# Four small copies moved from ACT and DVE to SP's DMA queue, with a new written order for every engine

## The chip, the core and the metric

The kernel runs on one core of a Trainium2 chip. The core has TensorE (PE), VectorE (DVE), ScalarE (ACT), GpSimd (POOL) and SyncE (SP); each runs its own list of instructions in order, and they wait for one another by semaphores. POOL and SP issue DMA transfers, which 16 DMA engines carry out. The metric is the device time of one execution in microseconds (us), less is better. Before the change it is 137.15 us, the median of 3 runs (137.09 to 137.99).

## The reference

Eight batches, eight heads, 576 positions, head size 64. Attention with a sliding window of 128 and a bias that falls with distance, then a token mixer whose mixing matrix is made from its input:

```
scores = scale * q @ k.T                       # per batch and head
scores = where(0 <= i - j < 128, scores - slope[h] * |i - j|, -1e9)
x      = softmax(scores) @ v                   # heads side by side: x is 576 x 512 per batch
wq, wk = x @ w_q, x @ w_k                      # 576 x 64 each
mixed  = (wq @ wk.T / 8) @ x
out    = relu(mixed) @ w_out                   # 576 x 512 per batch, float32
```

## The kernel before

All work is cut into named steps, and the kernel's text `ORDER` lists 720 of them as `name:engine`, for PE with the PSUM bank that the step fills and in some places a number of filler matmuls. The list was written by a planner from an estimated duration of each step per engine (the `on` argument of `add`, pairs of occupancy and latency in us); when the kernel is built, the steps are simply emitted in this order, and each engine executes its own in that order. So `ORDER` sets which engine does a step that several could do, which bank it uses, and in what order POOL and SP issue transfers.

A batch b goes through these steps (the first number is the batch):

- Loads: Lq, Lk, Lv, Lt (rows 512 to 575 of q and k), weights Lwq, Lwk, Lwo, all by POOL, which casts float32 to float16 on the way; FQ0 and FQ1 are the first two loads, by SP, cast by CQ0 and CQ1. The `load` function makes a load wait until only about 6 us of estimated service lie ahead of it.
- TW, TN, TT: transpositions of q and k on PE, evicted by ETW, ETN, ETT on ACT or DVE.
- QK: scores of a group of heads and a block of keys into a pair of PSUM banks; EXP: the exponential, on ACT, 64 times; MUL: the product with the exponential of the bias (zero outside the window), on DVE. Five buffers hold exponentials (`NPT = 5`).
- PV: the product with v and a column of ones; X: division by the sum (a reciprocal and a product), on DVE.
- XT and EXT: x is transposed and evicted (XT.0 and XT.1 large, XT.2 the last 64 rows). WK, WQ: the two projections, evicted by EWK, EWQ.
- G: since (wq wk.T) x = wq (wk.T x), only G = wk.T x (64 x 512) is made. It comes out as 128 partitions x 256: the lower 64 partitions hold columns 0 to 255, the upper 64 columns 256 to 511. EG copies it to `gs`. GX makes `gx`, the same with the two halves of the partitions exchanged, in two copies of 64 x 256.
- MX.0 and MX.1 multiply with `gs`, MX.2 and MX.3 with `gx`; RM is the relu and the scale, on ACT or DVE; OUT.0 to OUT.4 are the products with w_out, EO their evictions, DO the stores, by POOL or SP. The first store of SP after the step HOLD waits until the fourth last load has landed.

GX is the step that the change moves. In the function `add_g` (lines 727 to 771) its body already has a branch for each engine:

```
for r in range(2):
    out_ap = gx_s[b % 2][64 * r:64 * r + 64, :]
    lo = slice(64 - 64 * r, 128 - 64 * r)
    if o.eng == "SP":
        hold(nc.sync.dma_start(out=out_ap, in_=gs_s[b % 2][lo, :]))
    ...
    else:
        cp(o.eng, out_ap, one(g.bank)[lo, 0:256])
```

ACT and DVE copy from PSUM (line 222 or 224 of `cp`), SP would copy from `gs` in SBUF by DMA. The other lines that matter: L608 is EXP, L621 MUL, L662 and L663 X, L775 and L777 RM on ACT and DVE, L228 and L230 the evictions of transpositions, L494 and L496 those of TW, L213 the loads, L216 the stores, L908 the filler matmuls.

Of the kernel before, what the change touches and what calls it, by code (L numbers as in the profile page):

```python
# [48 lines left out]
QK1.1.0:P:1 QK0.3.1:P:3:1:0 QK0.3.0:P:0 Lv0.0:G zerop:G MUL0.1.0:V MUL0.0.0:V Lv0.1:G Lv0.2:G
Lv0.3:G EXP0.3.1:A Lv0.4:G MUL0.3.1:V EXP1.0.0:A EXP0.3.0:A Lq2.1:G ones4:V TW1.1:P:3 PV0.0:P:2  # L50
ones3:G ETW1.1.1:A X0.0:V ETW1.1.0:A PV0.1:P:0:1:0 MUL0.3.0:V EXP1.1.0:A Lk2.1:G QK1.0.1:P:3
EXP1.0.1:A Lwk:G Lv1.0:G X0.1:V PV0.2:P:2 X0.2:V QK1.1.1:P:1 EXP1.1.1:A PV0.3:P:0 X0.3:V
QK1.2.0:P:3 EXP1.2.0:A Lq2.0:G Lk2.0:G PV0.4:P:2 QK1.2.1:P:1 XT0.0:P:0 EXP1.2.1:A Lv1.1:G
XT0.1:P:3 EXT0.1:A X0.4:V XT0.2:P:20 EXT0.2:A EXT0.0:V MUL1.0:V QK1.3.1:P:0 EXP1.3.1:A TW2.1:P:1
# [12 lines left out]
PV2.4:P:1 MX1.3:P:2 RM1.3:A X2.4:V QK3.0.1:P:3 EXP3.0.1:A Lv3.1:G Lv3.0:G Lk4.2:G Lt2.3:G
Lk4.3:G Lv3.2:G PV2.2:P:0 QK3.1.1:P:2 EXP3.1.1:A X2.2:V XT2.2:P:10 EXT2.2:V TN4.1.0:P:3
ETN4.1.0:V Lk5.0:G Lq5.2:G Lq5.0:G Lk5.1:G Lv3.3:G Lv3.4:G Lk5.2:G MX1.2:P:0 RM1.2:A Lv4.2:G
Lk5.3:G Lq5.1:G Lq5.3:G XT2.1:P:1 QK3.3.0:P:2 EXP3.3.0:A Lq6.1:G Lv4.3:G QK3.2.1:P:3 QK3.2.0:P:0  # L70
EXT2.1:V WK2:P:10 EWK2:V MUL3.0:V EXP3.2.0:A QK3.3.1:P:2 EXP3.3.1:A WQ2:P:11 EWQ2:A G2:P:10
# [1 line left out]
EO0.0:A Lk6.2:G Lv5.4:G Lk6.1:G MUL3.1:V MX2.0:P:3 MX2.1:P:0 TN4.0.0:P:2 RM2.1:A RM2.0:A
ETN4.0.0:V OUT1.2:P:10 MUL3.3:V MX2.3:P:2 RM2.3:A QK4.0.1:P:0 EXP4.0.1:A Lk6.0:G TN4.0.1:P:3
ETN4.0.1:V OUT0.2:P:11 EO0.2:A PV3.0:P:2 MX2.2:P:3 RM2.2:A EO1.2:V QK4.0.0:P:0 EXP4.0.0:A
OUT1.0:P:10 X3.0:V EO1.0:A MUL3.2:V PV3.1:P:2 X3.1:V QK4.1.1:P:3 EXP4.1.1:A TN4.1.1:P:0 Lv5.0:G
Lt3.0:G Lq6.3:G MUL4.0:V ETN4.1.1:A OUT0.1:P:10 TT2:P:2 QK4.1.0:P:3 ETT5:V ETT4:V EO0.1:A
EXP4.1.0:A Lq6.2:G Lv6.4:G Lv5.3:G Lv5.2:G PV3.2:P:0 Lv5.1:G OUT2.2:P:10 EO2.2:A X3.2:V Lt3.2:G
Lq7.1:G TN5.1.0:P:3 ETN5.1.0:V Lk7.1:G Lq7.0:G DO0.1:G Lt3.1:G QK4.2.0:P:2 QK4.3.0:P:0 Lk7.3:G
Lq7.3:G Lt3.3:G PV3.3:P:1 EXP4.2.0:A X3.3:V EXP4.3.0:A OUT1.1:P:30 Lk7.0:G EO1.1:A PV3.4:P:2  # L80
MUL4.1:V QK4.3.1:P:0 EXP4.3.1:A XT3.0:P:1 EXT3.0:A X3.4:V OUT1.4:P:30 EO1.4:A MUL4.3:V
QK4.2.1:P:0 EXP4.2.1:A TN5.0.0:P:2 ETN5.0.0:V MUL4.2:V XT3.1:P:1 EXT3.1:A XT3.2:P:31 EXT3.2:A
OUT0.3:P:30 EO0.3:V TN5.1.1:P:0 ETN5.1.1:A TN5.0.1:P:2 ETN5.0.1:A QK5.0.0:P:1 EXP5.0.0:A
WK3:P:31 EWK3:V PV4.3:P:0 X4.3:V QK5.0.1:P:2 PV4.2:P:3 X4.2:V EXP5.0.1:A QK5.3.0:P:1 EXP5.3.0:A
# [8 lines left out]
X5.2:V QK6.1.1:P:3 EXP6.1.1:A WQ4:P:10 XT5.0:P:2 EWQ4:V EXT5.0:A QK6.2.0:P:0 EXP6.2.0:A
MX4.2:P:1 RM4.2:V XT5.1:P:3 EXT5.1:V OUT3.0:P:20 EO3.0:V MX4.0:P:0 MX4.1:P:1 RM4.1:V RM4.0:A
QK6.0.1:P:3 EXP6.0.1:A OUT3.3:P:21 EO3.3:V MX4.3:P:1 RM4.3:A Lv6.1:G TT3:P:0 ETT6:V ETT7:A
WK5:P:30 EWK5:A QK6.2.1:P:1 EXP6.2.1:A Lv6.0:G QK6.3.0:P:0 TN7.0.0:P:2 MUL6.1:V ETN7.0.0:V
# [7 lines left out]
MX5.2:P:2 RM5.2:A QK7.1.1:P:3 DO1.0:G EXP7.1.1:A XT6.2:P:00 HOLD:S DO1.1:S DO3.0:S DO4.0:S
EXT6.2:V MUL7.3:V OUT3.4:P:01 QK7.1.0:P:2 QK7.2.0:P:1 EXP7.1.0:A MUL7.0:V XT6.0:P:3 EXT6.0:A
OUT5.1:P:00 EXP7.2.0:A MUL7.1:V EO3.4:A PV7.4:P:2 X7.4:V EO5.1:A MUL7.2:V OUT5.2:P:30 EO5.2:A
OUT5.0:P:10 EO5.0:A WK6:P:00 EWK6:A PV7.0:P:3 DO2.0:S DO1.4:S X7.0:V PV7.1:P:2 X7.1:V DO4.3:G
# [836 lines left out]
```

## Time and profile before

| | |
|---|---|
| median of 3 runs | 137.15 us |
| the profiled execution | 137.09 us |
| its span, first to last instruction | 135.1 us |
| granted TensorE clock, mean | 0.99 |
| instructions | 5503 |
| busy: PE, ACT, DVE, POOL | 93%, 86%, 82%, 75% of the span |
| DMA | 24.86 MB moved, mean 184 GB/s |

A page of the profile shows one execution: each engine's busy time, the span in 40 slices with the busy share in tenths, the chain of work that ended last, the costliest groups of instructions with their mean duration and the idle time ahead of them, and the DMA issues with the time to landing. The trace answers finer questions: busy time in chosen stretches, timelines of one engine, who waited for whom.

### The profile page before, as it was taken

The numbers are of one execution on the slowest core, as the hardware profiler recorded it, in microseconds if no ns is written. First come the engines' busy times: TensorE is split into PE (matmuls) and PEld (weight loads), VectorE is DVE, ScalarE is ACT, GpSimd is POOL, SyncE is SP. The second block draws the span as 40 slices with busy tenths as digits, with TensorE's granted clock in tenths as the row PEclk, the third lists the DMA queues.
The fourth block names the chain that finished last, engine by engine and source line by source line (L and its number), as shares of the span: only waits on it lengthen the run. The fifth ranks groups of instructions, "written<-read, shape, count | busy, mean of one in ns | idle before, by whom it ended". The sixth has DMA issues, their size and how long they took to land.

```text
span 135.1 us, 5503 instructions
## 1 busy us (share of the span) xinstructions
PE 125.2 (93%) x2351; PEld 82.2 (61%) x2351; DVE 110.5 (82%) x210; ACT 116.6 (86%) x185; POOL 101.6 (75%) x154
## 2 busy tenths in 40 slices
...
DVE  5764869999899998999899999889998899936140
ACT  3489989999999999999999999999998996775710
...
GB/s 115 164 188 164 182 158 182 181 160 171 161 184 155 160 158 148 147 153 146 150 148 142 139 140 142 193 181 183 208 154 27 292 227 377 363 351 90 227 378 171
DMA packets 92680, 24.86 MB, mean 184 GB/s; under 512 B 80241, under 2 KB 89201, under 8 KB 92657
## 3 DMA queue, kind: packets, MB, share of 16 engines
...
q14 instruction: 6, 0.04, 0.1%
...
## 4 chain that ended last, share of the span: by engine, by line
PE 54%; POOL 18%; DMA 15%; ACT 6%; issue 3%; POOLq 0%; ACTq 0%
PE pair L207 48%; DMA natp<-in_k_dram 8%; PE pair L210 6%; POOL natp L213 5%; DMA vt<-in_v_dram 5%; POOL vt L213 5%; POOL natt L213 5%; ACT pt L608 4%; DMA wout_sb<-in_moe_w_out_dram 2%; POOL vt L332 1%; ACT natp L222 1%; ACT xT L228 0%; POOL vt L334 0%; POOL wq_sb L213 0%; POOL wout_sb L213 0%
## 5 line engine op out<-in xcount | busy, mean ns | idle before, releaser
L608 ACT ACTIVATE pt<-pair 128x1024 f16<-128x1024 f32 x64 | 63.7, 1045 | 1.9 <-PE pair L207 1.6
L621 DVE TENSOR_TENSOR pt<-pt,bias 128x2048 f16<-128x2048 f16 (+1 forms) x36 | 38.7, 1099 | 4.1 <-ACT pt L608 4.0
L213 POOL DMA_DIRECT2D vt<-in_v_dram x40 | 36.9, 1020 | 2.6 <-DMA natp<-in_k_dram 1.9
L207 PE MATMUL pair<-wout_sb,rm 128*128 128x512 f16 (+1 forms) x160 | 36.0, 381 | 0.1
L213 POOL DMA_DIRECT2D natp<-in_k_dram x24 | 23.8, 1006 | 1.1 <-POOLq L928 0.8
L216 POOL DMA_DIRECT2D out_dram<-natp x15 | 9.2, 618 | 20.3 <-ACT natp L222 20.3
L207 PEld LDWEIGHTS <-pt 128*128 128x128 f16 x576 | 20.4, 97 | 6.6 <-issue 3.4
L207 PE MATMUL pair<-qkT 64*128 64x256 f16 (+3 forms) x352 | 23.6, 243 | 0.7 <-DVE xT L230 0.2
L207 PE MATMUL pair<-vt,pt 128*128 128x65 f16 x576 | 23.3, 193 | 0.3
L663 DVE TENSOR_TENSOR x<-pair,inv 128x512 f16<-128x512 f32 x32 | 22.1, 691 | 1.1
L213 POOL DMA_DIRECT2D natp<-in_q_dram x23 | 22.2, 1010 | 0.5 <-DMA vt<-in_v_dram 0.5
L207 PEld LDWEIGHTS <-rm 128*128 128x128 f16 (+1 forms) x160 | 12.2, 100 | 12.9 <-issue 1.7
L775 ACT ACTIVATE rm<-pair 128x576 f16<-128x576 f32 x25 | 15.9, 660 | 1.9 <-PE pair L207 1.8
L222 ACT COPY natp<-pair 128x512 f32<-128x512 f32 x24 | 14.0, 607 | 3.6 <-PE pair L207 3.5
L210 PEld LDWEIGHTS <-natp 128*64 128x64 f16 (+1 forms) x512 | 12.9, 102 | 5.4 <-issue 3.9
L207 PEld LDWEIGHTS <-qkT 64*128 64x128 f16 x352 | 11.6, 94 | 5.3 <-issue 2.2
L908 PE MATMUL pair<-fill 128*128 128x512 f16 x31 | 10.5, 474 | 1.6 <-DVE fill L350 1.2
L210 PE MATMUL pair<-permh,natp 128*64 128x128 f16 x256 | 8.7, 220 | 1.3 <-ACT pt L608 0.9
L662 DVE RECIPROCAL inv<-pair 128x8 f32<-128x8 f32 (+1 forms) x40 | 8.1, 202 | 1.8 <-PE pair L207 1.5
L224 DVE COPY natp<-pair 128x512 f32<-128x512 f32 x8 | 5.5, 688 | 3.7 <-PE pair L207 3.6
L210 PEld LDWEIGHTS <-x 64*128 64x128 f16 x256 | 6.2, 114 | 2.2 <-issue 1.9
L210 PE MATMUL pair<-identh,x 64*128 64x64 f16 x256 | 7.1, 195 | 0.4 <-ACT pt L608 0.2
...
## 6 DMA issues: line engine op xcount, KB each, us to landing
vt<-in_v_dram POOLq DMA_DIRECT2D x32, 128.0 KB, 5.6
...
natp<-in_k_dram POOLq DMA_DIRECT2D x16, 128.0 KB, 5.3
natp<-in_q_dram POOLq DMA_DIRECT2D x16, 128.0 KB, 5.2
...
```

The costliest lines, as they stand in the source:

```text
L207: hold(nc.tensor.matmul(*a, **k))
L210: hold(nc.tensor.transpose(*a))
L213: hold(nc.gpsimd.dma_start(**k))
L216: i = (nc.gpsimd if eng == "POOL" else nc.sync).dma_start(**k)
L222: hold(nc.scalar.copy(out_ap, in_ap))
L224: hold(nc.vector.tensor_copy(out=out_ap, in_=in_ap))
L608: nc.scalar.activation(out=pt[:, 1024 * u:1024 * u + 1024], in_=two(s.bank).rearrange("p e c -> p (e c)"), func=AF.Exp, scale=SCALE)
L621: nc.vector.tensor_tensor(out=pt[:, lo:hi], in0=pt[:, lo:hi], in1=bt[:, lo:hi], op=ALU.mult)
L662: nc.vector.reciprocal(out=inv[r], in_=pxv[r, :, :, 64])
L663: nc.vector.tensor_tensor(out=x[r].rearrange("p (g h d) -> p g h d", g=2, h=4), in0=pxv[r, :, :, 0:64], in1=inv[r].unsqueeze(3).broadcast_ ...
L775: hold(nc.scalar.activation(out=out_ap, in_=in_ap, func=AF.Relu, scale=WSCALE))
L908: nc.tensor.matmul(where[:, half, :], fill[:, 0:P], fill, start=True, stop=True)
```

## The change

One duration is added, SP for GX, with 0.9 us of occupancy and 0.9 us of latency, and the whole order is a new one, worked out by the planner with it. GX of batches 1, 3, 4 and 5 goes to SP (two transfers of 64 partitions x 512 bytes each, SBUF to SBUF); the other four stay on ACT and DVE. The steps are the same 720. What else the new order gives to another engine, by count:

| step | ACT before, after | DVE before, after |
|---|---|---|
| GX | 5, 3 | 3, 1 |
| RM | 25, 18 | 7, 14 |
| ETN | 8, 13 | 8, 3 |
| EG | 5, 7 | 3, 1 |
| EWK | 6, 4 | 2, 4 |
| EO | 27, 26 | 9, 10 |
| ETW | 10, 11 | 6, 5 |
| ETT | 4, 5 | 4, 3 |
| EXT.0, EXT.1 (large) | 8, 7 | 8, 9 |
| EXT.2 (small) | 3, 6 | 5, 2 |
| ones, zerop (memsets) | 0, 0 | 3, 5 (POOL 3, 1) |

The filler matmuls go from 31 to 33. The order within each engine is new throughout: the loads' order, the banks, where stores stand between loads. The diff, cut to the lines with GX, the steps between EG3 and MX3.3, the start, the end, and the last loads:

```diff
@@ -40,79 +40,79 @@
...
-FQ1:S CQ1:A zeros:V ones0:V FQ0:S Lk0.0:G iota:G dist:V pads:V Lk0.1:G Lq0.1:G Lq1.0:G mask:G
-ident:G bias1:A CQ0:V ones2:V perm:V idh:V biasl1:V bias0:A ones1:G Lk1.0:G Lt0.2:G TW0.0:P:0:13
...
-QK2.1.1:P:1 MUL1.3:V G0:P:00 Lv1.2:G EG0:A GX0:A QK2.0.1:P:3 EXP2.0.1:A TW2.0:P:2 ETW2.0.0:A
...
-MUL2.1:V RM0.1:A RM0.3:A G1:P:30 TT1:P:2 ETT3:V EG1:A EWQ1:A ETT2:A MX0.2:P:0 RM0.2:V GX1:A
...
-EG2:V GX2:V Lv4.1:G EXP3.2.1:A OUT1.3:P:00 EO1.3:A Lv4.0:G Lv4.4:G Lk6.3:G Lq6.0:G OUT0.0:P:11
...
-TN6.0.0:P:0 GX3:V EXT4.0:V ETN6.0.0:A MUL5.1:V OUT2.3:P:20 EO2.3:A TN6.1.0:P:1 QK5.2.0:P:3
...
-MX3.3:P:0 RM3.3:A XT5.2:P:31 EXT5.2:V PV5.1:P:1 X5.1:V GX4:A QK6.1.0:P:2 EXP6.1.0:A PV5.2:P:0
...
-G5:P:30 EXP6.3.0:A WQ5:P:31 EWQ5:A TN7.0.1:P:2 EG5:V GX5:V ETN7.0.1:V TN7.1.0:P:1 ETN7.1.0:A
...
-OUT3.1:P:31 EO3.1:A X6.2:V PV6.1:P:0 QK7.3.0:P:1 EXP7.3.0:A DO3.1:G DO2.1:G X6.1:V QK7.2.1:P:2
...
-EXP7.0.0:A DO0.0:G DO3.2:G Lv7.1:G Lv7.2:G OUT4.1:P:01 EO4.1:A DO4.1:S XT6.1:P:1 EXT6.1:V
...
-DO1.3:G PV7.2:P:0 PV7.3:P:1 X7.3:V X7.2:V G6:P:30 WQ6:P:31 EWQ6:V EG6:A GX6:A DO5.2:G DO3.3:G
-OUT5.4:P:20 EO5.4:A XT7.0:P:1 EXT7.0:A XT7.1:P:0 EXT7.1:V DO0.3:G MX6.1:P:3 RM6.1:A XT7.2:P:21
-OUT5.3:P:20 EO5.3:A EXT7.2:V WK7:P:21 MX6.0:P:3 MX6.3:P:0 MX6.2:P:1 RM6.2:V WQ7:P:20 EWK7:A
-G7:P:21 EG7:V RM6.3:A RM6.0:A OUT6.3:P:30 DO4.2:S DO5.1:G EO6.3:V DO5.3:S OUT6.0:P:31 GX7:A
...
-OUT7.0:P:11 EO7.0:V DO7.0:S OUT7.4:P:30 EO7.4:A DO7.4:S
+FQ1:S FQ0:S Lk0.0:G CQ1:A ones4:V ident:G iota:G dist:V zerop:V zeros:V CQ0:V idh:V perm:V
+Lq0.1:G mask:G bias0:A Lk0.1:G bias1:A ones1:V TW0.0:P:0:15 ETW0.0.0:A ETW0.0.1:V
...
+EG0:A GX0:A Lt1.1:G MX0.0:P:3 RM0.0:V Lt1.3:G MUL1.2:V MX0.1:P:0 ETW2.1.1:A ETW2.1.0:A MX0.2:P:2
...
+QK3.0.1:P:1 EXP3.0.1:A Lk4.1:G Lk4.0:G PV2.1:P:0 X2.1:V QK3.0.0:P:3 GX1:S EXP3.0.0:A Lwo.0:G
...
+EXP3.2.0:A GX2:V Lv3.3:G OUT0.3:P:21 EO0.3:A OUT1.3:P:10 EO1.3:A MX2.2:P:0 MX2.0:P:2 MUL3.3:V
...
+ETN5.0.1:V EXP5.0.0:A G3:P:11 EG3:A GX3:S MUL4.3:V Lq6.3:G Lv5.0:G WQ3:P:20 EWQ3:A Lv5.3:G
+Lq6.1:G Lq6.2:G Lv5.4:G Lq6.0:G Lk6.0:G TN5.1.1:P:0 Lv5.1:G Lv5.2:G ETN5.1.1:A Lk6.3:G Lt3.3:G
+QK5.0.1:P:1 XT4.0:P:3 EXT4.0:V PV4.2:P:2 QK5.1.0:P:0 X4.2:V EXP5.0.1:A PV4.4:P:3 X4.4:V
+EXP5.1.0:A QK5.2.1:P:1 EXP5.2.1:A PV4.3:P:2 X4.3:V QK5.1.1:P:0 EXP5.1.1:A QK5.3.1:P:3 EXP5.3.1:A
+OUT2.1:P:10 EO2.1:A MUL5.0:V MX3.0:P:0 RM3.0:V XT4.1:P:2 EXT4.1:A OUT0.1:P:11 XT4.2:P:10
+EXT4.2:A MX3.3:P:0 RM3.3:A MX3.1:P:3 RM3.1:A MUL5.1:V EO0.1:V QK5.2.0:P:2 EXP5.2.0:A WK4:P:10
+EWK4:V PV5.0:P:0 X5.0:V QK5.3.0:P:3 EXP5.3.0:A WQ4:P:10 MUL5.2:V G4:P:11 EG4:A GX4:S TN6.1.0:P:0
...
+ETN7.1.0:A EXP6.3.1:A OUT4.0:P:30 ETN7.1.1:A EO4.0:A QK7.0.1:P:1 EXP7.0.1:A GX5:S QK7.1.1:P:2
+EXP7.1.1:A X6.1:V XT6.0:P:0 MUL6.3:V OUT4.2:P:30 EO4.2:A DO3.0:G DO1.4:G EXT6.0:V DO0.1:S
+DO2.1:S PV6.2:P:1 X6.2:V QK7.1.0:P:0 EXP7.1.0:A PV6.3:P:2 X6.3:V QK7.3.0:P:3 PV6.4:P:1 X6.4:V
+EXP7.3.0:A OUT3.3:P:00 EO3.3:A XT6.1:P:3 EXT6.1:V MX5.1:P:2 QK7.2.0:P:1 RM5.1:V DO2.3:G
...
+EXP7.2.1:A QK7.0.0:P:2 EXP7.0.0:A WK6:P:00 Lv7.2:G DO0.0:G OUT4.3:P:01 EWK6:A DO3.3:G Lv7.0:G
...
+WQ6:P:00 G6:P:30 EG6:A EWQ6:A GX6:A DO2.0:S DO3.4:S DO1.1:S OUT5.4:P:10 DO1.3:G EO5.4:A DO5.4:G
...
+EO5.3:A PV7.2:P:2 MUL7.3:V DO0.3:G DO4.3:G PV7.3:P:1 PV7.4:P:3 X7.0:V X7.2:V OUT4.1:P:00
+OUT5.0:P:01 X7.3:V XT7.1:P:1 X7.4:V EO4.1:A DO4.1:S DO1.2:G EO5.0:A DO5.0:G XT7.0:P:2 EXT7.0:V
+EXT7.1:A MX6.2:P:3 XT7.2:P:00 EXT7.2:A OUT5.1:P:01 EO5.1:A DO5.1:S DO5.3:G DO4.0:G DO5.2:G
+RM6.2:V WK7:P:20 EWK7:V MX6.0:P:3 MX6.1:P:1 RM6.0:A RM6.1:A MX6.3:P:0 RM6.3:V WQ7:P:21 G7:P:20
+EWQ7:A EG7:A GX7:A OUT6.3:P:10 EO6.3:A OUT6.1:P:21 MX7.3:P:0 MX7.1:P:1 MX7.0:P:3 OUT6.2:P:20
...
+DO6.2:S DO7.3:S EO7.1:V DO7.1:S DO7.0:S DO7.2:S OUT7.4:P:31 EO7.4:A DO7.4:S
...
@@ -768,7 +768,7 @@
...
-        gxs[b] = add(f"GX{b}", {**EV(0.53, 0.666), "POOL": (0.6, 0.65)}, [g, egs[b], *old], evx, frees=[g])
+        gxs[b] = add(f"GX{b}", {**EV(0.53, 0.666), "POOL": (0.6, 0.65), "SP": (0.9, 0.9)}, [g, egs[b], *old], evx, frees=[g])
...
```

More of the change, by code (lines that the diff above doesn't have):

```diff
@@ L49 @@
[L49 to L54, printed above, removed]
@@ L67 @@
[L67 to L71, printed above, removed]
-EG2:V GX2:V Lv4.1:G EXP3.2.1:A OUT1.3:P:00 EO1.3:A Lv4.0:G Lv4.4:G Lk6.3:G Lq6.0:G OUT0.0:P:11
@@ L73 @@
[L73 to L84, printed above, removed]
@@ L85 @@
-PV4.1:P:0 QK5.2.1:P:2 EXP5.2.1:A X4.1:V PV4.4:P:3 DO0.2:G Lq7.2:G QK5.3.1:P:1 EXP5.3.1:A X4.4:V
-XT4.1:P:0 EXT4.1:A MUL5.0:V Lk7.2:G OUT2.0:P:20 EO2.0:A PV4.0:P:3 X4.0:V QK5.1.1:P:1 EXP5.1.1:A
-TN6.1.1:P:0 ETN6.1.1:A G3:P:21 EG3:A MUL5.3:V WQ3:P:20 EWQ3:A QK5.1.0:P:1 EXP5.1.0:A XT4.0:P:3
-TN6.0.0:P:0 GX3:V EXT4.0:V ETN6.0.0:A MUL5.1:V OUT2.3:P:20 EO2.3:A TN6.1.0:P:1 QK5.2.0:P:3
-EXP5.2.0:A XT4.2:P:00 EXT4.2:V OUT2.1:P:01 EO2.1:A ETN6.1.0:V PV5.0:P:2 X5.0:V Lv6.3:G Lv6.2:G
-DO2.3:G MX3.2:P:3 MUL5.2:V TN6.0.1:P:1 RM3.2:A ETN6.0.1:A WK4:P:01 EWK4:A MX3.1:P:2 RM3.1:A
@@ L91 @@
-MX3.0:P:3 RM3.0:A QK6.0.0:P:1 PV5.4:P:0 X5.4:V EXP6.0.0:A PV5.3:P:2 X5.3:V G4:P:30 EG4:A
-MX3.3:P:0 RM3.3:A XT5.2:P:31 EXT5.2:V PV5.1:P:1 X5.1:V GX4:A QK6.1.0:P:2 EXP6.1.0:A PV5.2:P:0
[L93 to L96, printed above, removed]
@@ L103 @@
-EXP7.0.0:A DO0.0:G DO3.2:G Lv7.1:G Lv7.2:G OUT4.1:P:01 EO4.1:A DO4.1:S XT6.1:P:1 EXT6.1:V
[L104 to L107, printed above, removed]
-DO1.3:G PV7.2:P:0 PV7.3:P:1 X7.3:V X7.2:V G6:P:30 WQ6:P:31 EWQ6:V EG6:A GX6:A DO5.2:G DO3.3:G
@@ new lines @@
+EO2.2:A X3.4:V MUL4.0:V PV3.3:P:3 X3.3:V TN5.1.0:P:2 ETN5.1.0:A QK4.2.0:P:1 XT3.2:P:01
+EXP4.2.0:A EXT3.2:A OUT1.4:P:00 EO1.4:V TN5.0.0:P:2 ETN5.0.0:A TT2:P:3 ETT4:V ETT5:A XT3.0:P:1
+EXT3.0:A MUL4.2:V MUL4.1:V XT3.1:P:0 EXT3.1:A QK4.3.1:P:2 QK4.3.0:P:3 EXP4.3.1:A EXP4.3.0:A
+OUT2.0:P:10 PV4.0:P:0 X4.0:V WK3:P:11 PV4.1:P:2 X4.1:V EWK3:A EO2.0:A QK5.0.0:P:3 TN5.0.1:P:0
+ETN5.0.1:V EXP5.0.0:A G3:P:11 EG3:A GX3:S MUL4.3:V Lq6.3:G Lv5.0:G WQ3:P:20 EWQ3:A Lv5.3:G
+Lq6.1:G Lq6.2:G Lv5.4:G Lq6.0:G Lk6.0:G TN5.1.1:P:0 Lv5.1:G Lv5.2:G ETN5.1.1:A Lk6.3:G Lt3.3:G
@@ new lines @@
+QK5.0.1:P:1 XT4.0:P:3 EXT4.0:V PV4.2:P:2 QK5.1.0:P:0 X4.2:V EXP5.0.1:A PV4.4:P:3 X4.4:V
[3 more added lines that the diff above has]
+EWK4:V PV5.0:P:0 X5.0:V QK5.3.0:P:3 EXP5.3.0:A WQ4:P:10 MUL5.2:V G4:P:11 EG4:A GX4:S TN6.1.0:P:0
+ETN6.1.0:A MX3.2:P:2 TN6.0.0:P:3 ETN6.0.0:A OUT1.1:P:11 EWQ4:V MUL5.3:V MX4.1:P:3 RM4.1:V
@@ new lines @@
+QK6.0.1:P:0 RM3.2:A EO1.1:A PV5.2:P:2 X5.2:V PV5.1:P:1 X5.1:V EXP6.0.1:A TN6.0.1:P:3 ETN6.0.1:A
+Lq7.2:G Lk6.2:G Lt3.1:G Lv6.0:G Lk7.1:G QK6.0.0:P:0 EXP6.0.0:A Lt3.0:G Lq7.1:G PV5.3:P:2 X5.3:V
+OUT3.2:P:30 EO3.2:V TN6.1.1:P:0 ETN6.1.1:A QK6.1.0:P:1 EXP6.1.0:A XT5.1:P:2 EXT5.1:V PV5.4:P:3
+X5.4:V Lq7.0:G Lt3.2:G XT5.0:P:0 QK6.1.1:P:2 EXT5.0:V Lq7.3:G EXP6.1.1:A OUT3.0:P:10 XT5.2:P:11
+MX4.0:P:3 MX4.3:P:0 MUL6.0:V Lk7.3:G Lk7.2:G EXT5.2:A RM4.3:V Lk7.0:G EO3.0:A QK6.2.1:P:2
+RM4.0:A EXP6.2.1:A OUT3.1:P:11 EO3.1:V WK5:P:10 EWK5:A TT3:P:0 ETT7:A Lv6.1:G ETT6:A MX4.2:P:3
@@ new lines @@
+RM4.2:V QK6.2.0:P:2 EXP6.2.0:A Lv7.3:G PV6.0:P:1 X6.0:V DO1.0:G DO3.2:G Lv6.2:G Lv6.3:G Lv6.4:G
+OUT2.3:P:01 EO2.3:V QK6.3.0:P:3 EXP6.3.0:A TN7.0.0:P:2 TN7.0.1:P:1 ETN7.0.1:A ETN7.0.0:A
+MUL6.1:V WQ5:P:00 EWQ5:V G5:P:01 TN7.1.0:P:3 QK6.3.1:P:1 TN7.1.1:P:2 EG5:V MUL6.2:V PV6.1:P:0
+ETN7.1.0:A EXP6.3.1:A OUT4.0:P:30 ETN7.1.1:A EO4.0:A QK7.0.1:P:1 EXP7.0.1:A GX5:S QK7.1.1:P:2
+EXP7.1.1:A X6.1:V XT6.0:P:0 MUL6.3:V OUT4.2:P:30 EO4.2:A DO3.0:G DO1.4:G EXT6.0:V DO0.1:S
+DO2.1:S PV6.2:P:1 X6.2:V QK7.1.0:P:0 EXP7.1.0:A PV6.3:P:2 X6.3:V QK7.3.0:P:3 PV6.4:P:1 X6.4:V
```

56 lines of the change are left out of this document (35 added, 21 removed).

## The prediction

> **What bounds the kernel now.** I read the page first: the engines' shares, the slices, the chain of work that ended last.
>
> ```profile
> PE 125.2 (93%) x2351; PEld 82.2 (61%) x2351; DVE 110.5 (82%) x210; ACT 116.6 (86%) x185; POOL 101.6 (75%) x154
> ...
> DVE  5764869999899998999899999889998899936140
> ACT  3489989999999999999999999999998996775710
> ...
> PE 54%; POOL 18%; DMA 15%; ACT 6%; issue 3%; POOLq 0%; ACTq 0%
> ```
>
> The first line is each engine's busy time and share; in the digits one slice is 3.4 us. Five engines are nearly full, and an average over the span can't say which one sets the pace. So I cut the span at the end of ACT's last exponential (111.3), the end of DVE's last normalisation (117.1) and the last matmul (130.3), and read each stretch.
>
> ```profile
> core 0: us, PE busy (x) PEld busy (x) DVE busy (x) ACT busy (x) POOL busy (x), PEclk, DMA share, GB/s
> 25.00:111.30 86.30, 84.52 (x1776) 58.83 (x1776) 80.92 (x135) 84.52 (x131) 75.98 (x98) 1.00 1.92 163
> 111.30:117.10 5.80, 5.80 (x124) 4.50 (x122) 5.54 (x13) 3.63 (x10) 3.19 (x6) 1.00 1.13 369
> 117.10:130.30 13.20, 13.12 (x126) 6.39 (x120) 6.55 (x12) 8.23 (x17) 0.57 (x1) 1.00 0.74 258
> ```
>
> In the long stretch ACT is idle 86.30 - 84.52 = 1.8 us and DVE 86.30 - 80.92 = 5.4 us. Every group of scores goes ACT (exponential), DVE (product), PE (PV), DVE (normalisation), so the two work as a relay, ACT with next to no air and DVE with 6%. From 111.3 to 117.1 DVE alone is full (5.54 of 5.80). After that comes a chain of short steps that no engine fills except PE.
>
> PE looks just as full, but its instructions overlap in the records: its weight loads fill only 58.83 of 86.30. The Trainium skill, "Perfetto Trace Analysis", Identifying the Most-Contended Engine, says the same: matmul busy share is no measure of how near TensorE is to its limit, LDWEIGHTS share is. By that rule PE isn't the bound here, and the rival below that makes it the bound gets less chance.
>
> The sum is made against the profiled execution: 137.09 us, of which 135.1 is span and 2.0 lies around it. The median of the three runs is 137.15, so the two are one number.
>
> **Part 1, the copies that leave ACT and DVE.** GX1 and GX4 leave ACT, GX3 and GX5 leave DVE. What a pair of copies holds its engine for is read in the timelines of ACT and DVE (start, length, instruction), from its start to the next instruction's.
>
> ```profile
> 40.38 0.74 ACT L222 CAST gx<-pair 64x256 f16<-64x256 f32 x2
> 41.14 0.58 ACT L494 COPY qkT<-pair 128x512 f32<-128x512 f32 x1
> ...
> 95.84 0.86 DVE L224 CAST gx<-pair 64x256 f16<-64x256 f32 x2
> 96.73 0.69 DVE L230 COPY qkT<-pair 128x1024 f16<-128x1024 f16 x1
> ...
> 87.61 1.94 ACT L608 ACTIVATE pt<-pair 128x1024 f16<-128x1024 f32 x2
> ```
>
> ACT: 41.14 - 40.38 = 0.76 each, 1.5 for two. DVE: 96.73 - 95.84 = 0.89 each, 1.8 for two. The last row gives the overlap of neighbours: two exponentials of 1.045 take 1.94, so one holds ACT for 0.90. The PSUM bank of G also comes free with EG alone, 0.76 or 0.89 sooner at four places; no wait for it shows, so I cost that at 0, at best -0.8 once.
>
> **Part 2, the new division of the other evictions.** Counting the engine letters of the two orders: ACT loses 7 RM, 2 EWK, 1 EO, gains 5 ETN, 2 EG, 1 ETW, 1 ETT, and in EXT gives one large and takes three small; DVE mirrors this, and takes two memset steps from POOL (ones, zerop).
>
> The groups of instructions, shape by shape (count, busy us, mean ns of one, idle time before it):
>
> ```profile
> L608 ACT ACTIVATE pt<-pair 128x1024 f16<-128x1024 f32 x64 | 63.7, 1045 | 1.9 <-PE pair L207 1.6
> L775 ACT ACTIVATE rm<-pair 128x576 f16<-128x576 f32 x25 | 15.9, 660 | 1.9 <-PE pair L207 1.8
> L777 DVE TENSOR_SCALAR rm<-pair 128x576 f16<-128x576 f32 x7 | 5.3, 751 | 2.5 <-PE pair L207 2.5
> L228 ACT COPY qkT<-pair 128x512 f32<-128x512 f32 x8 | 4.7, 600 | 0.0
> L230 DVE COPY qkT<-pair 128x1024 f16<-128x1024 f16 x8 | 5.5, 688 | 0.3 <-PE pair L210 0.2
> L222 ACT CAST gs<-pair 128x256 f16<-128x256 f32 x5 | 2.0, 394 | 1.9 <-PE pair L207 1.9
> L224 DVE CAST gs<-pair 128x256 f16<-128x256 f32 x3 | 1.3, 422 | 0.4 <-PE pair L207 0.4
> L222 ACT CAST wkn<-pair 128x320 f16<-128x320 f32 x6 | 2.6, 439 | 0.0
> L224 DVE CAST wkn<-pair 128x320 f16<-128x320 f32 x2 | 1.0, 486 | 0.8 <-PE pair L207 0.8
> L228 ACT COPY xT<-pair 128x128 f32<-128x128 f32 x3 | 1.0, 336 | 0.0
> L230 DVE COPY xT<-pair 128x256 f16<-128x256 f16 x5 | 1.4, 280 | 0.0
> L621 DVE TENSOR_TENSOR pt<-pt,bias 128x1024 f16<-128x1024 f16 x8 | 5.3, 687 | 4.0 <-ACT pt L608 4.0
> L332 DVE MEMSET vt<- 64x264 uint32 x3 | 0.8, 278 | 0.3
> ```
>
> ACT, each row less 0.13 of overlap (that of the exponentials is 1.045 - 0.90 = 0.145, that of the gx pair less): RM -7 x 0.53 = -3.7; ETN +5 x 0.47 = +2.35; EG +2 x 0.26 = +0.5; EWK -2 x 0.31 = -0.6; three small EXT +0.6; the rest (one ETW and one ETT more, one EO and one large EXT fewer; all 0.25 to 0.5) about -0.2. That is -1.0, with the copies -2.5 us. DVE, each less 0.08: RM +7 x 0.67 = +4.7; ETN -5 x 0.61 = -3.0; EG -2 x 0.34 = -0.7; EWK +2 x 0.41 = +0.8; three small EXT -0.6; the rest +0.3. That is +1.5, with the copies -0.3; the two memset steps (0.28 by the last row and a few much shorter ones each) add under 1 us, in the first 20 us, where DVE waits for ACT in any case: the eight half-width products, all of batch 0, have 4.0 us of idle time before them (last row but one). So ACT gets 2.5 us lighter and DVE stays as it is, both within about 0.7.
>
> Before the first exponential nothing is gained: the same five transfers (FQ0, FQ1, Lk0.0, Lk0.1, Lq0.1) come ahead of the second transposition in both orders. I cost the start at 0, between -0.5 and +0.5.
>
> **Part 3, the copy on SP.** SP has only its two first loads before the stores near the end, so the four copies stand behind nothing; behind GX5 stand the stores DO0.1 and DO2.1, which nobody waits for. No copy from SBUF to SBUF is in this trace. The nearest transfers are SP's loads in its timeline, and two rows of the list of DMA issues (last column: median us from issue to landing):
>
> ```profile
> 0.74 0.96 SPq L400 DMA_DIRECT2D natp<-in_q_dram  x2
> ...
> out_dram<-natp SPq DMA_DIRECT2D x6, 128.0 KB, 2.8
> out_dram<-natp POOLq DMA_DIRECT2D x2, 128.0 KB, 6.3
> ```
>
> Two issues take 0.96, and a landing comes 2.8 to 6.3 after its issue, the second issue standing 0.5 behind the first: ready 3.3 to 6.8 us after EG. I take 3.3, because it is SP's own row, though those stores ran after the loads had ended. What covers it: for GX3, the nearest case, ACT has EWQ3, ETN5.1.1, five exponentials, EO2.1 and two EXT between EG3 and the first reader MX3.3, with the 0.90 above 4.5 + about 2.0 = 6.5 us; GX4 and GX5 have 6.6 and 8.1, GX1 over 10. So the copy costs nothing up to 6.5, and at the long end 6.8 - 6.5 = 0.3 each time, with all of PE's later work queued behind the waiting MX. Four times 64 KB are 0.26 MB beside 24.86 moved in all, 1%. The Trainium skill, "DMA: Bandwidth & Descriptors", Anatomy of one DMA, speaks against such copies: about 2.0 us are fixed per DMA however small it is. By it an estimate is 2.1 us plus the issue: under the cover, so it would take the late copy's chance away. No run here shows a small copy.
>
> **Part 4, the end.** The end in the timelines of DVE and PE, and the last links of the chain of waits, follows below. PE has the same matmuls after the last normalisation in both orders (ten output tiles, the last projections and mixes), and the last step stays OUT7.4, its eviction by ACT and two stores by SP.
>
> ```profile
> 116.43 0.69 DVE L663 TENSOR_TENSOR x<-pair,inv 128x512 f16<-128x512 f32 x1
> 117.04 0.45 DVE L224 CAST wqT<-pair 128x288 f16<-128x288 f32 x1
> 117.67 0.89 DVE L230 COPY xT<-pair 128x1024 f16<-128x1024 f16 x2 [0.19 <-PE pair L210]
> ...
> 118.87 0.75 PE L207 MATMUL pair<-wk_sb,xT 128*128 128x64 f16 x20
> ...
> 121.25 8.99 PE pair L207 x48
> 130.24 0.02 issue
> 130.26 0.58 ACT natp L222
> ```
>
> Now the last normalisation (X7.2, ends 117.12) is followed by a large transposition, its eviction and a small one, both on DVE, and WK7 starts at 118.87, 1.75 later. In the new order X7.4 is last, which feeds only the small transposition; EXT7.1 and EXT7.2 go to ACT, EXT7.0 (0.69) to DVE, and one output tile (about 0.9) lies between: about 1.2. That is -0.5, between -0.8 and 0. From WK7 on the chain is as long as it was (8.99 of matmuls to 130.24).
>
> **The sum.** The relay to the last normalisation: if ACT alone set its pace -2.5, if DVE alone 0; half, -1.25, since each waits for the other. End -0.5. Against this I set +0.45 for stalls of an order that the trace hasn't seen, an estimate: a quarter of ACT's present 1.8. Together -1.3: 137.09 - 1.3 = 135.8.
>
> **The rivals.** (a) ACT is the whole bound: its 1.8 us of idle time speak for it, DVE's full stretch before 117.1 against. Then -2.5 - 0.5: 134.1. (b) DVE or PE is the bound: DVE's load is unchanged and 5.54 of 5.80 full where the batches end; PE's 84.52 of 86.30 says PE, its weight loads say no. Then the gain is used up as idle time on ACT, the end's 0.5 is half lost: 136.9. (c) Late copies: 0.3 at each of four places, 1.2 on top of the forecast: 137.0. (d) Slower: a store ahead of the last loads in POOL's queue (POOL's and PE's timelines, the list of DMA issues).
>
> ```profile
> 103.44 1.09 POOL L216 DMA_DIRECT2D out_dram<-natp  x2 [5.82 <-ACT natp L222]
> ...
> 105.59 1.82 POOL L213 DMA_DIRECT2D vt<-in_v_dram  x2
> ...
> 112.94 1.87 PE L207 MATMUL pair<-vt,pt 128*128 128x65 f16 x56
> ...
> vt<-in_v_dram POOLq DMA_DIRECT2D x32, 128.0 KB, 5.6
> ```
>
> Now POOL stands 5.82 us for an eviction, then issues two loads of batch 7's V at 105.59. In the new order Lv7.0 and Lv7.4 stand behind DO3.3, which waits for EO3.3 on ACT. If that ends at about 103, as the eviction that frees POOL does now, the store takes 0.54, Lv7.0 goes out at about 103.9 and lands 5.6 later, at 109.5. PV7.0, which starts at 112.94 now, wants it some 2 us sooner, at 111. So it decides if that eviction ends later than 104.5; each us beyond then costs one at PV7.0, with four normalisations in a row behind it. 2.5 us beyond give +2.5, less 0.5 at the end: 139.1.
>
> **How the numbers follow.** Forecast 0.42 (own range 135.0 to 136.6), (a) 0.19, (b) 0.21, (c) 0.04, (d) 0.14. A measurement of this kernel tells about 1% from no change: below 135.8 is faster, above 138.5 slower. Faster: (a) and half of the forecast, 0.40. Slower: (d), 0.14. Same: the rest, 0.46. The range holds all but (d) and reaches to the low end of (a): 134.0 to 138.4.
>
> **What would show it.** Right: gx on ACT three times two and on DVE once two; ACT busy about 2.5 us less over the span and idle more than 1.8 us in the long stretch; DVE busy within 1 us of 110.5; the last normalisation at about 116; WK7 some 1.2 us after it. Wrong: a wait of a weight load or matmul for gx by DMA (c); POOL idle before DO3.3 beyond 104.5 and PE waiting for vt (d); DVE without gaps and the last normalisation at 117 (b), at 114.6 (a).

## The result, and the profile after

| | before | after |
|---|---|---|
| median of 15 runs each | 137.66 us | 136.65 us |
| lowest to highest | 137.02 to 139.38 | 135.30 to 137.41 |
| the profiled execution, its span | 137.09, 135.1 | 136.72, 134.9 |

The ratio is 0.9928, 95% interval 0.9904 to 0.9952: 1.0 us faster (0.7 to 1.3). A few executions ran clearly longer than the others of their kernel, and the ratios leave them out. With more runs the median of the kernel before is 137.66; the profiled 137.09 was its third shortest of 15 executions, while 136.72 is an ordinary one of the changed kernel. So the two profiles lie only 0.37 apart, and 0.6 of the 1.0 can't be placed by setting one trace against the other. That is what most of the experiments are for.

From the page of the changed kernel: busy time and share of each engine, the slices of DVE and ACT (one is 3.4 us), and the chain that ended last by engine.

```profile
PE 124.2 (92%) x2353; PEld 81.9 (61%) x2353; DVE 110.0 (82%) x216; ACT 114.8 (85%) x182; POOL 101.0 (75%) x144
...
DVE  3654989899999967988999999999998997973600
ACT  3767978999999989999999999979999897478450
...
PE 65%; ACT 10%; DVE 9%; issue 7%; DMA 4%; POOL 1%; POOLq 0%; DVEq 0%
```

ACT is 116.6 - 114.8 = 1.8 us lighter, DVE as heavy as before. POOL and DMA, a third of the chain before, have nearly gone from it, and PE has 65% instead of 54%.

The same three stretches as before, busy time of each engine (columns: stretch, length, PE, PEld, DVE, ACT, POOL with the count of instructions, then clock, DMA share, GB/s).

```profile
25.00:111.30 86.30, 84.15 (x1806) 59.01 (x1805) 81.32 (x132) 83.21 (x130) 75.05 (x101) 1.00 1.96 172
111.30:117.10 5.80, 5.59 (x88) 3.68 (x88) 4.94 (x11) 3.24 (x7) 2.70 (x5) 1.00 0.89 304
117.10:130.30 13.20, 13.20 (x135) 6.66 (x134) 6.70 (x10) 8.46 (x17) 2.66 (x5) 1.00 0.76 281
```

In the long stretch ACT is now idle 86.30 - 83.21 = 3.1 us where it was 1.8: 1.3 us of what it lost came back as idle time. DVE is idle 5.0 (5.4 before).

The groups that moved, shape by shape, and then everything that touches `gx`, both of the changed kernel.

```profile
L775 ACT ACTIVATE rm<-pair 128x576 f16<-128x576 f32 x18 | 11.4, 668 | 0.9 <-PE pair L207 0.8
L222 ACT CAST gs<-pair 128x256 f16<-128x256 f32 x7 | 2.9, 410 | 0.0
L777 DVE TENSOR_SCALAR rm<-pair 128x576 f16<-128x576 f32 x14 | 10.4, 752 | 3.3 <-PE pair L207 2.6 <-ACT gs L222 0.5
```

```profile
L764 SPq DMA_DIRECT2D gx<-gs x8: 461/536/604, 41.8 to 98.3; - x8
L222 ACT CAST gx<-pair x6: 363/366/369, 30.0 to 122.3; 64x256 f16<-64x256 f32 x6
L224 DVE CAST gx<-pair x2: 419/422/425, 54.0 to 54.4; 64x256 f16<-64x256 f32 x2
its engine sat idle before it (us, times) until:
  issue: 2.6, 6
  ACT qkT L494: 0.5, 1
  DVE gx L224: 0.4, 1
...
DMA to landing us min/median/max: 3.4/4.3/5.0
```

The second fence gives for each form the least, median and greatest duration in ns. Eight transfers of 32 KB replace four pairs of copies; each took 3.4 to 5.0 us from its issue to its landing, and among the releasers of those that read `gx` there is no DMA: no reader waited for a transfer.

The end, in the timelines of DVE and of PE (start, length), and the last links of the chain.

```profile
117.12 0.69 DVE L663 TENSOR_TENSOR xtl<-pair,inv 64x512 f16<-64x512 f32 x1
118.00 0.69 DVE L230 COPY xT<-pair 128x1024 f16<-128x1024 f16 x1 [0.18 <-PE pair L210]
```

```profile
118.23 1.04 PE L207 MATMUL pair<-wout_sb,rm 128*128 128x512 f16 x4
119.11 0.75 PE L207 MATMUL pair<-wk_sb,xT 128*128 128x64 f16 x20
```

```profile
111.51 5.80 PE pair L207 x88
...
118.30 12.12 PE pair L207 x96
130.41 0.02 issue
130.44 0.58 ACT natp L222
```

The last normalisation ends at 117.12 + 0.69 = 117.81 (117.12 before), WK7 starts at 119.11, 1.30 later (1.75 before), and every link of the chain from 111.51 to the last matmul at 130.4 (130.2 before) is PE.

Then comes the last eviction with its stores. Here is the stretch from its start to the end of the span, first before, then after (columns as above):

```profile
130.26:135.10 4.84, 0.00 (x0) 0.00 (x0) 0.00 (x0) 0.58 (x1) 0.00 (x0) 0.73 0.68 237
130.44:134.90 4.46, 0.00 (x0) 0.00 (x0) 0.00 (x0) 0.58 (x1) 0.00 (x0) 1.00 0.54 166
```

In these two profiles the new order starts its last eviction 0.18 us later and still ends 0.2 sooner. Less is left to store by then: 4.84 us at 237 GB/s are 1.15 MB, 4.46 us at 166 GB/s are 0.74 MB. This stretch takes 4.76 to 4.91 us in the five profiles of the old order (with those of the experiments below) and 4.45 to 4.77 in the nine of the new one. The time around the span falls as well: 1.91 to 2.04 us in every execution of the old order whose span is on record, 1.72 to 1.86 in every one of the new order. So about 0.5 of the 1.0 us lies behind the last matmul or outside the span. That the first part comes from the smaller rest of stores is argued and not tried; where the second comes from isn't known.

### The profile page after: what moved, and what is told of

Same layout as the page of the kernel before. It is cut to its first block, busy times and chain, and to the rows that moved or that the text cites. A ratio compares the mean times of both kernels' runs of the same rounds, so it can differ in the third digit from the quotient of the medians.

```text
span 134.9 us, 5537 instructions
## 1 busy us (share of the span) xinstructions
PE 124.2 (92%) x2353; PEld 81.9 (61%) x2353; DVE 110.0 (82%) x216; ACT 114.8 (85%) x182; POOL 101.0 (75%) x144
## 4 chain that ended last, share of the span: by engine, by line
PE 65%; ACT 10%; DVE 9%; issue 7%; DMA 4%; POOL 1%; POOLq 0%; DVEq 0%
PE pair L207 53%; PE pair L210 11%; ACT pt L608 5%; DMA natp<-in_k_dram 4%; DVE x L663 3%; DVE pt L621 2%; ACT rm L775 1%; DVE rm L777 1%; ACT qkT L494 1%; DVE inv L662 1%; DVE xtl L663 1%; ACT gs L222 1%; DVE gx L224 1%; ACT wkn L222 1%; ACT gx L222 1%
## 5 line engine op out<-in xcount | busy, mean ns | idle before, releaser
L207 PE MATMUL pair<-vt,pt 128*128 128x65 f16 x576 | 23.8, 193 | 1.0 <-issue 0.5
L213 POOL DMA_DIRECT2D natp<-in_k_dram x24 | 23.1, 1009 | 1.6 <-POOLq L928 0.8
L222 ACT COPY natp<-pair 128x512 f32<-128x512 f32 x22 | 13.2, 600 | 6.7 <-PE pair L207 6.7
L207 PEld LDWEIGHTS <-qkT 64*128 64x128 f16 x352 | 12.7, 94 | 6.3 <-issue 3.1
L777 DVE TENSOR_SCALAR rm<-pair 128x576 f16<-128x576 f32 x14 | 10.4, 752 | 3.3 <-PE pair L207 2.6
L775 ACT ACTIVATE rm<-pair 128x576 f16<-128x576 f32 x18 | 11.4, 668 | 0.9 <-PE pair L207 0.8
L908 PE MATMUL pair<-fill 128*128 128x512 f16 x33 | 10.5, 453 | 1.7 <-DVE fill L350 1.2
L228 ACT COPY qkT<-pair 128x512 f32<-128x512 f32 (+1 forms) x18 | 9.2, 542 | 0.8 <-PE pair L210 0.6
L494 ACT COPY qkT<-pair 128x512 f32<-128x512 f32 x11 | 6.2, 593 | 2.2 <-PE pair L210 2.1
```

Source lines behind the costliest of these rows:

```text
L207: hold(nc.tensor.matmul(*a, **k))
L213: hold(nc.gpsimd.dma_start(**k))
L222: hold(nc.scalar.copy(out_ap, in_ap))
L775: hold(nc.scalar.activation(out=out_ap, in_=in_ap, func=AF.Relu, scale=WSCALE))
L777: hold(nc.vector.tensor_scalar(out=out_ap, in0=in_ap, scalar1=0.0, scalar2=WSCALE, op0=ALU.max, op1=ALU.mult))
L908: nc.tensor.matmul(where[:, half, :], fill[:, 0:P], fill, start=True, stop=True)
```

## The experiments

All twelve ran in five rounds each beside the kernel before, in three groups; ratios are to the kernel before, with 95% intervals. Where a kernel is compared with the changed one, the two ratios are divided and their intervals joined as independent errors. The theory was that of the prediction: the freed engine time is the gain, about half of it through the relay of ACT and DVE. The rivals: the new order gains without the copies, or the copies gain without the new order, or another engine holds the time whatever ACT does.

**The copies alone, in the old order.** The four steps get the letter S where they stand, and the order stays.

```diff
-MUL2.1:V ... G1:P:30 ... EG1:A EWQ1:A ETT2:A MX0.2:P:0 RM0.2:V GX1:A
+MUL2.1:V ... G1:P:30 ... EG1:A EWQ1:A ETT2:A MX0.2:P:0 RM0.2:V GX1:S
# in the same way GX3:V, GX4:A, GX5:V become :S
```

> The order of before, with GX1, GX3, GX4 and GX5 given to SP at their places and nothing else changed. In the trace of before the first reader of each (MX.2 or MX.3) starts 6.9, 3.3, 2.9 and 3.1 us after EG; in the trace of the changed kernel such a copy has landed 4.0 to 5.6 us after EG. Theory (the order had to be made for the copy): GX1 is covered, the other three are late by 1 to 2.3 us each with PE queued behind them, against 0.8 us gained on each engine: 0.5 to 3 us slower than before. Rival (the copies are the gain and the order is incidental): about 1 us faster than before, as the changed kernel is.

Measured: 1.0369 (1.0324 to 1.0414), 5.1 us slower. The waits for `gx` in it (us in total, times, longest), and the time that its copies took:

```profile
PEld L207 <- DMA gx<-gs: 4.9, 5, 1.6
PE pair L207 <- DMA gx<-gs: 3.9, 5, 1.5
...
DMA to landing us min/median/max: 1.8/4.6/5.4
```

The second row is the matmuls behind the weight loads of the first, so these are the same five waits: 4.9 us in which PE stands for the transfers, where the changed kernel has no such wait. The granted clock of this profile was 0.976 against 0.990 before, so the length of the waits is rough. In the old order the first reader comes 2.9 to 3.3 us after EG for batches 3, 4 and 5 (end of EG to start of MX, in the trace of before), and a copy takes longer than that. In the changed kernel the same distances are 6.2, 8.2 and 8.6, and the copy is in `gx` 4.0 to 5.6 us after EG. So the move to SP needs the new order.

**The new order, with the copies back on their engines.** All four stand right behind EG, on the engine they had; then the two of ACT and the two of DVE alone.

```diff
-G1:P:10 EG1:A Lv2.4:G ...
+G1:P:10 EG1:A GX1:A Lv2.4:G ...
-EG5:V MUL6.2:V ...
+EG5:V GX5:V MUL6.2:V ...
# likewise EG3:A GX3:V and EG4:A GX4:A; the four GX:S go
```

> The new order, with all four copies back on ACT (GX1, GX4) and DVE (GX3, GX5), each right behind its EG. Relay theory: half of the 1.5 us on ACT and of the 1.8 us on DVE comes back, +1.6 against the changed kernel, ratio to before about 1.005. Rival (the gain is the new order alone): no change against the changed kernel, ratio 0.993. Second rival (ACT or DVE alone is the bound): +1.5 or +1.8, told apart by the next two runs.

> The new order with only GX1 and GX4 back on ACT (1.5 us more on ACT). Relay: +0.75 us against the changed kernel. ACT the bound: +1.5. DVE the bound: 0, because ACT idles 3 us between 25 and 111 us in the changed kernel.

> The new order with only GX3 and GX5 back on DVE (1.8 us more on DVE). Relay: +0.9 us against the changed kernel. DVE the bound: +1.8, and the last normalisation 1.8 later than 117.8. ACT the bound: 0.

Measured: all four 1.0177 (1.0139 to 1.0214), that is 3.4 ± 0.6 us above the changed kernel and 2.4 above the one before. The two of ACT 1.0055 (1.0031 to 1.0078), +1.75 ± 0.5 on the changed kernel; the two of DVE 1.0127 (1.0097 to 1.0157), +2.75 ± 0.5. With the copies where they were, the new order is the worse one; it seems to have spent the time that they leave. The copies of each engine cost at least what they hold it for (1.5 and 1.8 in the prediction), on ACT and on DVE alike. The two costs add up to 4.5 ± 0.7, the two together cost 3.4 ± 0.6, so they may partly cover each other.

**Engine time or PSUM bank.** A copy of G holds an engine, and also the bank of G. Here the changed kernel keeps its transfers, and spare copies of the same size, from SBUF into a buffer that nothing reads, stand where the copies stood.

```diff
+        for r in range(2):
+            h = slice(64 * r, 64 * r + 64)
+            cp(o.eng, scr[o.eng][h, :], wm[h, :])
...
-EG1:A Lv2.4:G
+EG1:A SX1:A Lv2.4:G
# likewise SX3:V behind GX3:S, SX4:A behind GX4:S, SX5:V behind EG5:V
```

> The changed kernel as it is, with the copies on SP, and four pairs of spare copies of the same size on ACT (batches 1, 4) and DVE (3, 5), at the places where the run before had the four copies back. They read a constant in SBUF and write a scratch tile that nobody reads, so they cost engine time but hold no PSUM bank. If the 3.4 us that the four copies cost in the new order are engine time, this is as slow: ratio to before about 1.018. If a part of them is G's PSUM bank, which the copies keep from PE until they end, this is faster than that: with half of the engine time (relay), +1.6 against the changed kernel, ratio about 1.005.

> The same with the two spare pairs on DVE alone. Engine time: as slow as with GX3 and GX5 back on DVE, ratio 1.013 (2.8 us over the changed kernel for 1.8 us of DVE). PSUM bank: clearly under that, +0.9 to +1.8 against the changed kernel, ratio 0.999 to 1.006.

Measured: 1.0172 (1.0126 to 1.0218) with all four, the same as with the copies themselves (1.0177); 1.0087 (1.0053 to 1.0121) with DVE's two, +2.2 ± 0.6 against +2.75 ± 0.5 of the real copies. So the cost of all four is engine time, within ± 0.8 us. Whether the bank adds something on DVE's side isn't settled: 0.4% lies between two intervals that overlap.

**No copy at all, in either order.** The four GX are left out, and MX.2 and MX.3 of these batches read `gs`, so the result lacks that part of the mixing.

```diff
-        g, w = (gs_s, gx_s)[j // 2][b % 2], wqT_s[b % 2]
+        g, w = (gs_s, gs_s if b in (1, 3, 4, 5) else gx_s)[j // 2][b % 2], wqT_s[b % 2]
```

> The order of before, with GX of batches 1, 3, 4 and 5 left out altogether: MX.2 and MX.3 of these batches multiply with gs in place of gx, so that part of the mixing is not the reference's. What the four copies cost in the old order, with no transfer to wait for. If they cost there what they cost in the new one, 3.4 us: ratio 0.975, and the new order gives 2.4 of them away to cover the transfers. If the new order is as good as the old one apart from the copies: ratio 0.993, 1 us.

> The changed kernel with the four transfers on SP left out in the same way (MX.2 and MX.3 of batches 1, 3, 4, 5 multiply with gs). If the transfers are covered, as their landing 4.0 to 5.6 us after EG against covers of 6.3 to 10.9 says: no change against the changed kernel, ratio 0.993. If they cost something (DMA share, late landing): below 0.990.

Measured: the old order without them 0.9979 (0.9952 to 1.0005), 0.3 us faster (-0.1 to 0.7); the new order without its transfers 0.9927 (0.9895 to 0.9958), where the changed kernel has 0.9928. So the transfers cost nothing that can be measured (± 0.4%), and in the old order the 3.3 us of ACT and DVE are worth about a tenth of that, 0.7 us at most. The first stretch of the old order without copies shows where they go:

```profile
25.00:111.30 86.30, 84.41 (x1777) 58.76 (x1777) 79.82 (x132) 83.45 (x128) 76.14 (x98) 1.00 1.94 165
```

Against the kernel before ACT falls from 84.52 to 83.45 and DVE from 80.92 to 79.82, both into idle time; PE stays at 84.4 to 84.5. This is the clearest word against the relay: both of its engines got lighter, and half of that, 1.6 us, did not come.

**Does PE set the pace?** Eight filler matmuls of 128x512 (L908) stand before eight QK steps of batches 4 to 7, in both orders. Nothing reads what they compute.

```diff
-QK4.1.1:P:3 EXP4.1.1:A
+QK4.1.1:P:3:1 EXP4.1.1:A
# likewise QK4.2.0, QK5.0.1, QK5.2.1, QK6.0.0, QK6.1.1, QK6.2.1, QK7.0.1
```

> The order of before with one more filler matmul (512 columns, about 0.21 us of PE) ahead of each of eight QK steps between batches 4 and 7, 1.7 us of PE work that nobody uses. Leaving the four copies out gained only 0.2% in this order, and in its trace PE has no wait of over 0.3 us between 50 and 117 us. If PE sets the pace of the old order, all of it shows: +1.7 us, ratio 1.012. If ACT and DVE set it and PE has air (its steps at their fastest fill 86% of that stretch): under 0.5 us, ratio below 1.004.

> The same eight filler matmuls in the changed kernel, whose 3.3 us of copies or spare copies cost 3.4. If its pace is ACT's and DVE's alone: under 0.5 us, ratio to before below 0.997. If PE paces it as well (all three in one ring): +1.7, ratio 1.005.

Measured: in the old order 1.0136 (1.0086 to 1.0187), +1.9 us (1.2 to 2.6); in the new one 1.0097 (1.0065 to 1.0128), +2.3 ± 0.55 on the changed kernel. A filler writes into the PSUM bank of the QK step behind it, so one might think that it waits for that bank and delays QK although PE has time. The row of the eight in the old order (last column: idle time before them) says otherwise:

```profile
L908 PE MATMUL pair<-fill 128*128 128x512 f16 x8 | 3.1, 382 | 0.0
```

None of them waited, in the new order neither. What one adds is read from the start of PV before it to the start of QK behind it, for example 59.33 to 59.90 without and 59.29 to 60.09 with the filler: 0.23, for eight 1.8 us. Here are the first stretch of the old order with fillers and of the new one with fillers:

```profile
25.00:111.30 86.30, 84.65 (x1761) 57.91 (x1761) 79.47 (x134) 82.96 (x128) 76.09 (x98) 1.00 1.90 157
```

```profile
25.00:111.30 86.30, 83.92 (x1771) 57.74 (x1766) 78.94 (x129) 80.97 (x126) 75.24 (x101) 1.00 1.95 168
```

ACT's busy time in the stretch falls from 84.52 to 82.96 and from 83.21 to 80.97: it waits while PE does the added work. PE has no room for these 1.8 us in either order, although its weight loads fill only 58 of 86 us.

**Is there room for more on ACT and DVE in the old order?** The old order keeps its copies and gets the four spare pairs as well.

```diff
-GX1:A
+GX1:A SX1:A
# likewise GX3:V SX3:V, GX4:A SX4:A, GX5:V SX5:V
```

> The order of before with its four copies, and four more spare pairs on the same engines right behind them (3.3 us, from SBUF to a scratch tile). In the new order the same addition cost 3.4 us. If the old order has air on ACT and DVE (leaving copies out gained 0.3 us): about as little, under 1 us, ratio below 1.007. If every engine is as tight there as in the new order and only taking away doesn't help, because the next wait is at hand: +3 us, ratio 1.022.

Measured: 1.0306 (1.0243 to 1.0369), +4.2 us (3.3 to 5.1) for spare copies that keep ACT and DVE busy for these times (line numbers one higher, since a line was added):

```profile
L225 DVE CAST ident<-wm 64x256 f16<-64x256 f32 x4 | 1.9, 472 | 0.1
L223 ACT CAST scr<-wm 64x256 f16<-64x256 f32 x4 | 1.6, 403 | 0.1
```

That is 3.5 us. Taking 3.3 us from these places gave 0.3, putting 3.5 there costs 4.2. The old order is tight on PE and on ACT and DVE at once: more on PE, or more on ACT and DVE together, shows in full, and less on ACT and DVE shows hardly.

**The store ahead of the last loads.** In the changed kernel DO3.3 stands before Lv7.0 and Lv7.4 in POOL's queue, the place of the slower rival. POOL's timeline in the changed kernel, then PV7.1 in PE's and the normalisation behind it in DVE's:

```profile
105.32 0.57 POOL L216 DMA_DIRECT2D out_dram<-natp  x1 [3.84 <-ACT natp L222]
105.87 1.63 POOL L213 DMA_DIRECT2D vt<-in_v_dram  x2
```

```profile
111.51 0.90 PE L207 MATMUL pair<-vt,pt 128*128 128x65 f16 x24 [0.42 <-ACT wqT L222]
```

```profile
112.26 0.21 DVE L662 RECIPROCAL inv<-pair 128x8 f32<-128x8 f32 x1 [0.68 <-ACT gx L222]
```

POOL stood 3.84 us for EO3.3, and Lv7.0 went out at 105.87. It landed at 111.37 and PV7.1 started at 111.51, after 0.42 us in which PE stood. Both rows name steps of ACT that ended just before, but PV7.1 doesn't read `wqT`, and the normalisation doesn't read `gx`: it reads what PV7.1 makes. The experiment puts the store behind the two loads:

```diff
-... EWK6:A DO3.3:G Lv7.0:G
-MX5.3:P:3 RM5.3:A MX5.0:P:1 Lv7.4:G RM5.0:A
+... EWK6:A Lv7.0:G
+MX5.3:P:3 RM5.3:A MX5.0:P:1 Lv7.4:G DO3.3:G RM5.0:A
```

> The changed kernel with the store DO3.3 behind Lv7.0 and Lv7.4 in POOL's queue instead of ahead of them. In its trace POOL waits 3.84 us for EO3.3, the load Lv7.0 goes out at 105.87 and the step PV7.1 that needs it starts at 111.51, while DVE idles 0.68 before X7.1. Theory (the load is late, the prediction's rival d in small): -0.6 us against the changed kernel, ratio 0.988. Rival (PE and the end hide it): no change, 0.993.

Measured: 0.9927 (0.9894 to 0.9960), the time of the changed kernel. POOL, PE and DVE in it:

```profile
102.82 1.57 POOL L213 DMA_DIRECT2D vt<-in_v_dram  x2 [1.18 <-DMA vt<-in_v_dram]
105.21 1.13 POOL L216 DMA_DIRECT2D out_dram<-natp  x2 [0.82 <-ACT natp L222]
```

```profile
110.91 0.91 PE L207 MATMUL pair<-vt,pt 128*128 128x65 f16 x24
```

```profile
111.67 0.21 DVE L662 RECIPROCAL inv<-pair 128x8 f32<-128x8 f32 x1 [0.21 <-PE pair L207]
```

The loads went out 3 us sooner, PE no longer stood before PV7.1, the idle time before that normalisation fell from 0.68 to 0.21, and the last matmul of this profile ended at 129.83, 0.58 sooner. The median didn't move (± 0.55 us on the changed kernel). So one execution agrees with the theory and the twelve together don't show it; a gain of up to about 0.5 us isn't excluded. No version beat the changed kernel.

## Why the prediction was right, and where not

**The time.** Forecast 135.8, measured 136.65. Of the 0.85 between them, 137.66 - 137.09 = 0.57 is the base: I set the profiled execution equal to the median of three runs, and with fifteen the median lies higher. The gain itself was forecast at 1.3 and measured at 1.0 (0.7 to 1.3).

**Part 1** (a pair of copies holds ACT for 0.76, DVE for 0.89) sized the work well on ACT, where putting two back into the new order costs 1.75 ± 0.5 for 1.5. On DVE it costs 2.75 ± 0.5 for 1.8, so a copy there is worth more than the time that it holds the engine. The bank at 0: spare copies that leave the bank alone cost the same as all four, so this stood, but for the open 0.4% on DVE.

**Part 2** (ACT -2.5, DVE as it is): measured 116.6 to 114.8, -1.8, and 110.5 to 110.0, both within the margin of 0.7, ACT at its edge.

**Part 3** (the copy on SP costs nothing): right. I took 3.3 us after EG; it was 4.0 to 5.6, between the ends 3.3 and 6.8. The cover worked out for GX3 was 6.5; the trace has 6.2. The Trainium skill, "DMA: Bandwidth & Descriptors", Anatomy of one DMA, gives the fixed part of about 2.0 us for DMAs that GpSimd issues; these copies were issued by SP and mostly took longer. One landing in the old order took 1.8 us, the median of eight was 4.3 in the changed kernel and 4.6 in the old order. The old order with the copies on SP, where readers come after 2.9 to 3.3 us, is rival (c) in earnest: 5.1 us slower, where the prediction priced lateness at 0.3 a time.

**Part 4** (the end, -0.5): WK7 comes 1.30 after the last normalisation, 0.45 sooner than the 1.75 of before; 1.2 was forecast. But nothing waits in this distance: PE runs through it without a break in both orders, so the chain of short steps that the prediction costed isn't what the end consists of. And "From WK7 on the chain is as long as it was", with 2.0 us kept around the span, put at nothing the two places where about 0.5 us was gained: the stores behind the last matmul and the time around the span.

**The sum's first term failed**: "if ACT alone set its pace -2.5, if DVE alone 0; half, -1.25". The last normalisation was forecast at about 116 and came at 117.81, 0.7 later than in the trace of before, though ACT was lighter (0.6 of this may be the choice of the two executions); in the old order 3.3 us less on both engines gave 0.3. Nothing like half arrives through this relay. Two earlier steps stand behind it. "From 111.3 to 117.1 DVE alone is full" misses the first number of the same row: PE was busy for 5.80 of 5.80 us there, as it was for 84.52 of 86.30 and 13.12 of 13.20 in the other two. And "By that rule PE isn't the bound here" set PE aside. It is drawn from the rule of the Trainium skill ("Perfetto Trace Analysis", Identifying the Most-Contended Engine) that the weight-load share tells how near TensorE is to its limit. The measurement decides against it here: with that share at 58.83 of 86.30, eight more matmuls cost 1.9 us in the old order and 2.3 in the new. The chain of waits before had it too, ahead of the links that the prediction shows:

```profile
89.60 0.46 PE pair L210 x15
90.06 0.03 issue
90.08 2.82 PE pair L207 x18
...
109.34 7.49 PE pair L207 x130
```

From 89.60 to the last matmul at 130.24 it consists of PE alone, but for 0.1 us of issue. The mechanism of rival (b), PE or DVE as the bound and ACT's gain used up as idle time (1.8 to 3.1), describes the long stretch better than the forecast does. Its gain doesn't: 137.09 - 136.9 = 0.2, where 1.0 was measured and 1.3 forecast.

So the right total comes from a wrong split, and that is luck: of the forecast -1.3, -0.8 was to come through the relay, less the stalls, and hardly any of it did, while about 0.5 came where the sum has no term. What the runs show in place of the split: neither part gains by itself (the copies alone +5.1, the order alone +2.4, no copies in the old order -0.3), and both together give -1.0. The longer distance from EG to MX in the new order hides the transfers, and its other moves seem to have used the 3.3 us that left ACT and DVE. Which of them bring the gain isn't known; none was tried singly. One place to look is PE's own order: by the two pages PE is busy 1.0 us less (125.2 us for 2351 matmuls, 124.2 for 2353), with the same steps.

**Rival (d)** was half right. EO3.3 did end after its threshold of 104.5, at about 105.0, and POOL did stand for it; by its rule that costs 0.5 us, not the 2.5 that it was priced at. Lv7.0 landed 0.14 us before PV7.1 started, and PE had stood 0.42 us. The last experiment removed this wait; its profile was shorter by about the 0.5, its median was not, so the price lies between nothing and 0.5.

**Open**: why adding costs in full what taking away doesn't give back. That the removed time runs into the next wait on PE fits the filler runs and the chain, but less work on PE wasn't tried, so it is argued and not shown. Open too is why an ordinary execution of the kernel before is 0.6 us longer than its profiled one.
